# A hand-written first stage: statistics straight through on VectorE, its filler matmuls and GpSimd scalings left out

## The chip, the cores and the metric

The kernel runs on one core of one Trainium2 chip. Times are device microseconds of one execution; a number for a kernel is the median of its runs. In the profile, PE is TensorE's matmuls and PEld its weight loads, DVE is VectorE, ACT is ScalarE, POOL is GpSimd and SP is the engine that issues most transfers.

## What is computed

A linear attention without softmax, normalised by its root mean square, and then an MLP mixer, all in fp32 (8 batches, 8 heads, 576 positions, head size 64; 256 token and 1536 channel features):

```python
kv  = np.einsum('bhsd,bhse->bhde', k, v)
out = np.einsum('bhsd,bhde->bhse', q, kv)
rms = np.sqrt(np.mean(out * out, axis=-1, keepdims=True) + 1e-06)
x   = out / rms * g_norm                      # then (B,H,S,D) -> (B, S, H*D)

h   = np.maximum(x.transpose(0, 2, 1) @ w_tok1, 0.0) @ w_tok2
u   = x + h.transpose(0, 2, 1)
out = u + np.maximum(u @ w_ch1, 0.0) @ w_ch2
```

The MLP weights come as 64-bit floats, which the kernel decodes to fp32 itself.

## The kernel before

**Stages.** Two batches make a pair, and there are four pairs. A first stage (the list `start`) does the attention of pair 0 and begins its token mixing. `middle` and two `steady` stages each interleave the attention of the next pair with the token mixing of the one before; `last` does the token mixing of pair 3. After that comes the channel MLP, by far the longest part, as an unbroken row of matmuls (ps_a, ps_b, ps_d and others), with fast matrix multiplication in sums and differences on VectorE.

**Order of the work.** The order is written out by hand. Each string of `start` is a list of step names, and `play` (L1192) calls them one after another; each call records instructions, and every engine executes its own in the order in which they were recorded. Instructions of different engines wait for one another by semaphores where they share data or a buffer. A name in a list is a letter and numbers:

- `kvSH`: k by v of side S (the batch within the pair), half H (four heads), 20 matmuls of 64 columns into ps_kv; `eSH`: its eviction to kvp (`evict`, L379 to 385). In pair 0 the eviction takes the whole 128x256 (the banks were zeroed ahead, so that two heads make a block-diagonal square) on VectorE, L383; in later pairs two 128x128 halves go on ScalarE, L130.
- `aCT`: attend, four matmuls q by kv of column group C (0 and 1 are side 0, 2 and 3 side 1, 4 the remainder of both), tile T of 128 positions, into ps_o (ps_r for the remainder), of which there are two banks.
- `gCT`: gain, VectorE, L444: x = bank times g_norm. `qCT`: square of the same bank, ScalarE, L448. `tCT`: sum over each head, VectorE, L465. `mC`: mean and epsilon, VectorE, L470. `rC`: root, ScalarE, L475. `iC`: inversion with one refining step, four small VectorE instructions, L479 to 484. The two readers of a bank, gain and square, stand in the order in which they were recorded: the second waits for the first.
- Scaling x by the inverse, in three forms: `sCT` on ScalarE (eight activations of 128x64, L498), `dCT` on VectorE (one, L502), `pCT` on GpSimd (one, L506).
- `h0TJ`: one matmul of token mixing's first product, 128x512 into ps_h, of side 0, feature half T, position tile J (tile J is x of group J // 2, tile J % 2). In `middle`, `h1T` are the four of side 1 at once, `hr` those of the remainder, `uI` the second product and its addition.
- `wNK`: steps of decoding a token weight; `lSH`, `lqS`, `lrS`: loads for the next pair; `jN`: N matmuls of the identity whose result nobody reads (`keep_warm`, ps_j; TensorE's pace in the first microseconds is lower).

All matmuls are recorded through one helper, L133; a matmul in fp32 shows as two records in the profile. Copies by ScalarE show as L130, transfers as L121. The steps that the change touches are the strings of `start`, `evict`, and the sizes for which `jN` exist; the second stage, whose first steps wait for x of groups 2 to 4, is the same text before and after.

**Transfers.** Loads go on SP's queue in recorded order; an issue waits for the eighth one ahead of it to have landed, and for the buffer (k and v of a pair's four parts have one buffer each, q two).

Of the kernel before, what the change touches and what calls it, by code (L numbers as in the profile page):

```python
# [20 lines left out]
def kernel(  # L21
# [90 lines left out]
    def do(f, *a, **kw):  # L112
        return lambda: f(*a, **kw)
# [15 lines left out]
    def copy(o, a):  # L129
        keep(nc.scalar.copy(o, a))  # L130
# [121 lines left out]
    def t_sums(b):  # L252

        def step(o, x, y):
            return lambda: tensor_add(b(o), b(x), b(y), ALU.subtract)

        return [step(5, 7, 1), step(6, 3, 5), step(7, 3, 7), step(4, 2, 6)]
# [96 lines left out]
    def attention(pair, groups):  # L354
# [7 lines left out]
        whole = pair == 0  # L362
# [16 lines left out]
        def evict(side, half):  # L379
            n = P if whole else D  # L380
            o, i = kvp[side][:, 2 * half:2 * half + 2, :n], kv_ps[side, half][:, :, :n]
            if whole:
                keep(nc.vector.tensor_copy(o, i))  # L383
            else:
                copy(o, i)
# [123 lines left out]
        for s in range(2):  # L509
            for h in range(2):  # L510
                steps |= {f"kv{s}{h}": do(kv, s, h), f"e{s}{h}": do(evict, s, h),
                          f"l{s}{h}": do(load, 4 * pair + 4 + 2 * s + h)}
            steps |= {f"lq{s}": do(load_q, 2 * pair + 2 + s), f"lr{s}": do(load_q_rest, 2 * pair + 2 + s)}
# [678 lines left out]
    def play(lines, after={}, **stages):  # L1192

        for name in " ".join(lines).split():
            if name.isdigit():
                for _ in range(int(name)):
                    next(stages["rounding"], lambda: None)()
            elif name[0] == "-":  # L1200
                stages["before"][name[1:]]()
            else:
                next(stages[s][name] for s in ("attention", "mixing", "more")
                     if name in stages.get(s, ()))()
# [28 lines left out]
    for block in tok1[2:] + tok2:  # L1233
# [6 lines left out]

    start = [
        "kv00 e00 l00 j14 w01 w11 w02 w03 w04 w12 w13 w14", "kv01 j10 e01 l01",
        "a00 g00 q00", "a01 g01 q01 t00", "a10 g10 q10 t01 m0 r0", "a11 g11 q11 t10 i0 p00 p01",
        "kv10 j6 t11 m1 r1 e10 i1 s10 p11", "kv11 j2 e11", "h000 h001 h002 h003", "a20 g20 q20", "a21 g21 q21 t20",
        "h010 t21 m2 r2", "a30 g30 q30 i2 p20", "a31 g31 q31 t30", "h011 t31 m3 r3 p21", "a40 i3 p30 g40 q40 p31",
        "h012 h013 t40 m4 r4 w21 i4 s40 lq0 l10 l11 lr0 lr1"]
    middle = [
        "kv00 e00 w31 w22 w23 w24", "h10 -lq1 w32 w33 w34", "kv01 e01 w41 w42",
        "h11 w43 w44", "hr l00", "a0 q00 g01 q01 g00 t00 t01", "u0 z2 f0", "u1 l01",
# [20 lines left out]
    more = {f"w{n}{k}": f for n, b in enumerate(tok1 + tok2) for k, f in enumerate(b)}  # L1270
# [6 lines left out]
    def keep_warm(n):  # L1277

        o = ps["h"].tile([P, DM], F32, name="ps_j", tag="h")
        for _ in range(n):  # L1280
            matmul(o[:, :P], lhsT=ident, rhs=ident, start=True, stop=True)

    more |= {f"j{n}": do(keep_warm, n) for n in (2, 6, 10, 14)}
    play(start, attention=attentions[0], mixing=mixings[0], more=more)
    play(middle, attention=attentions[1], mixing=mixings[0], before=attentions[0],
         more=more, rounding=rounding)
    for n in range(1, B // 2 - 1):
        play(steady[n - 1], attention=attentions[n + 1], mixing=mixings[n], before=attentions[n],
             more=more, rounding=rounding)
# [16 lines left out]
    more = {f"c{i}": f for i, f in enumerate(t_sums(lambda n: uT[0][:, SB[n]]))}  # L1306
# [97 lines left out]
```

## Time and profile before

| | us |
|---|---|
| median of 3 runs | 789.23 (788.98 to 789.61) |
| the profiled execution, its own time | 788.88 |
| span of its profile | 787.10 |
| TensorE busy in the span | 774.4 |
| VectorE busy | 612.9 |
| ScalarE busy | 265.4 |
| GpSimd busy | 78.3 |
| first stage ends on TensorE, next stage's first k by v starts | 39.79 |
| TensorE's last matmul ends | about 783.9 |

A line of a timeline reads: start in us from the span's start, length in us, engine, line, operation, what is written from what, sizes, how many; in brackets, how long the engine had been idle and what it waited for. A matmul's end is modelled, and matmuls overlap, so that start to start is the better measure of what one costs. A line of waits reads: who waited, for whom, us in total, how often, the longest. A line of stretches: the stretch and its length, then busy us (and instructions) of PE, PEld, DVE, ACT and POOL, the granted clock of TensorE, the mean share of 16 DMA engines, GB/s.

### The profile page before, as it was taken

Reading aid. Unit: us, or ns where it says so; the run is one execution under the profiler, and the core shown is the slowest. Engines: PE = TensorE matmul, PEld = TensorE weight load, DVE = VectorE, ACT = ScalarE, POOL = GpSimd, SP = SyncE. Lnnn points to the kernel's source line nnn. Section 1 sums busy time; section 2 is a strip of 40 time slices with the busy share of each in tenths; the row PEclk is TensorE's granted clock in tenths of the full one; section 3 lists DMA queues with packets and bytes.
Section 4 is the critical chain, followed back from the end, with each engine's and each line's share of the span. In section 5 each row is a group of like instructions: output and inputs, shape, how many; then the busy total and the mean of one; then the engine's idle time right before and its main releaser. Section 6 shows DMA issues by size and latency. Waiting matters only on the chain.

```text
span 787.1 us, 14853 instructions
## 1 busy us (share of the span) xinstructions
PE 774.4 (98%) x5832; PEld 652.6 (83%) x5832; DVE 612.9 (78%) x906; ACT 265.4 (34%) x513; POOL 78.3 (10%) x91
## 2 busy tenths in 40 slices
PE   6999999999999999999999999999999999999998
PEld 5655555544888888999988899998889999889998
DVE  2666887796776868988778889776898885787977
ACT  2356564846110133511133242123352113325211
POOL 1211212122410000010100001010000101000111
PEclk9999999999999999999999999999999999999999
DMA  9999999587699795599897579889559889655864
GB/s 295 327 334 371 361 371 344 212 268 282 235 292 337 269 339 148 154 309 205 246 236 231 151 218 272 247 203 290 148 158 283 206 222 230 200 153 151 200 173 91
DMA packets 132614, 192.12 MB, mean 244 GB/s; under 512 B 13633, under 2 KB 92225, under 8 KB 132545
## 3 DMA queue, kind: packets, MB, share of 16 engines
q1 hardware_dynamic: 115984, 167.54, 68.1%
q0 software_dynamic: 14656, 22.02, 13.7%
q10 hardware_dynamic: 1904, 1.61, 0.7%
q8 instruction: 46, 0.75, 0.4%
q14 instruction: 24, 0.19, 0.1%
HBM read 138.31 MB, written 52.82 MB: 243 GB/s over the span
## 4 chain that ended last, share of the span: by engine, by line
PE 95%; DVE 2%; ACT 1%; DMA 1%; issue 0%; SPq 0%; ACTq 0%
PE ps_d L133 28%; PE ps_b L133 19%; PE ps_a L133 19%; PE ps_h L133 8%; PE ps_u L133 8%; PE ps_v L133 5%; PE ps_c L133 3%; PE ps_kv L133 2%; PE ps_w L133 2%; PE ps_o L133 2%; DMA raw<-in_moe_w_tok_dram 1%; ACT x L498 1%; DVE x L444 0%; DVE ms L465 0%; PE ps_j L133 0%
## 5 line engine op out<-in xcount | busy, mean ns | idle before, releaser
L133 PE MATMUL ps_d<-ui,w 128*128 128x256 f32 x504 | 118.6, 379 | 0.0
L133 PEld LDWEIGHTS ps_d<-ui,w 128*128 128x128 f32 x504 | 95.1, 190 | 12.8 <-DVE v L124 0.2
L130 ACT COPY ps_d<-ps_a 128x768 f32<-128x768 f32 (+1 forms) x56 | 32.0, 571 | 215.6 <-PE ps_a L133 215.6
L124 DVE TENSOR_TENSOR v<-v,v 128x1536 f32<-128x1536 f32 (+2 forms) x70 | 103.5, 1483 | 0.3
L133 PE MATMUL ps_b<-w,sv 128*128 128x128 f32 x672 | 84.7, 276 | 0.0
L133 PE MATMUL ps_a<-w,v 128*128 128x128 f32 x672 | 84.2, 275 | 0.0
L133 PEld LDWEIGHTS ps_a<-w,v 128*128 128x128 f32 x672 | 79.9, 192 | 0.2
L133 PEld LDWEIGHTS ps_b<-w,sv 128*128 128x128 f32 x672 | 79.5, 192 | 0.2
L133 PE MATMUL ps_u<-h,w_tok 128*128 128x512 f32 (+1 forms) x160 | 67.2, 606 | 0.2
L133 PE MATMUL ps_d<-w,v 128*128 128x128 f32 x528 | 66.3, 275 | 0.0
L133 PE MATMUL ps_h<-x,w_tok 128*128 128x512 f32 (+1 forms) x160 | 65.5, 603 | 0.7 <-ACT x L498 0.7
L133 PEld LDWEIGHTS ps_d<-w,v 128*128 128x128 f32 x528 | 62.7, 192 | 0.3
L127 ACT ACTIVATE v<-v 128x768 f32<-128x768 f32 (+1 forms) x54 | 42.6, 821 | 55.1 <-DVE v L124 55.1
L133 PE MATMUL ps_d<-w,sv 128*128 128x128 f32 x480 | 60.1, 275 | 0.0
L133 PEld LDWEIGHTS ps_d<-w,sv 128*128 128x128 f32 x480 | 57.1, 192 | 0.2
L133 PEld LDWEIGHTS ps_h<-x,w_tok 128*128 128x128 f32 (+1 forms) x160 | 26.1, 189 | 32.7 <-issue 29.0
L1121 POOL DMA_DIRECT2D out_dram<-us x11 | 14.1, 1278 | 379.3 <-ACT us L130 347.4
L133 PEld LDWEIGHTS ps_u<-h,w_tok 128*128 128x128 f32 (+1 forms) x160 | 24.8, 179 | 31.0 <-issue 25.6
L133 PE MATMUL ps_a<-uT,w 128*128 128x256 f32 x192 | 46.7, 379 | 0.0
L444 DVE TENSOR_TENSOR x<-ps_o,g_sb 128x512 f32<-128x512 f32 x32 | 21.6, 687 | 28.6 <-PE ps_o L133 23.3
L133 PE MATMUL ps_b<-ui,w 128*128 128x256 f32 x168 | 40.8, 379 | 0.0
L133 PEld LDWEIGHTS ps_a<-uT,w 128*128 128x128 f32 x192 | 36.3, 190 | 4.8
(145 smaller groups left out, 1216.2 us busy)
## 6 DMA issues: line engine op xcount, KB each, us to landing
w<-parts SPq DMA_DIRECT2D x168, 384.0 KB, 4.1
w<-parts SPq DMA_DIRECT2D x56, 192.0 KB, 3.4
uT<-blocks SPq DMA_DIRECT2D x36, 256.0 KB, 5.7
k_in<-in_k_dram SPq DMA_DIRECT2D x16, 512.0 KB, 8.7
qT<-in_q_dram SPq DMA_DIRECT2D x8, 1024.0 KB, 9.2
out_dram<-x POOLq DMA_DIRECT2D x16, 512.0 KB, 6.1
v_in<-in_v_dram SPq DMA_DIRECT2D x14, 512.0 KB, 8.8
raw<-in_moe_w_ch_dram SPq DMA_DIRECT2D x8, 768.0 KB, 10.4
```

The lines of the kernel that those rows point to most:

```text
L124: keep(engine.tensor_tensor(out=o, in0=a, in1=b, op=op))
L127: keep(nc.scalar.activation(o, a, AF.Relu))
L130: keep(nc.scalar.copy(o, a))
L133: keep(nc.tensor.matmul(*a, **kw))
L444: keep(nc.vector.tensor_mul(x, bank[c, h], g_sb.to_broadcast([P, number(c), D])))
L498: keep(nc.scalar.activation(x[:, k, h], x[:, k, h], AF.Copy, scale=inv[:, k, h]))
L1121: keep(nc.gpsimd.dma_start(to.rearrange("t p e -> p t e"), a, accum_op=ALU.add))
```

## The change

- The second side's k by v (`e10`, `e11`) are evicted by ScalarE instead of VectorE, still as whole 128x256.
- In the first stage VectorE's instructions are recorded one pair of tiles after another, without those of the next between (gains, sums, mean, inversion, scaling), and from group 1 on with the square ahead of the gain of the same bank.
- Tiles 00 and 01 are both scaled by VectorE; in groups 1, 2 and 3 VectorE scales tile 0 and ScalarE tile 1. GpSimd scales none in this stage (seven before); ScalarE scaled 10 and 40 before, now 11, 21, 31 and 40.
- The filler `j6` and `j2` is gone; `j14` and `j10` stay.
- The first product's matmuls of the two feature halves are taken in turn, as each tile of x comes.

```diff
         def evict(side, half):
             n = P if whole else D
             o, i = kvp[side][:, 2 * half:2 * half + 2, :n], kv_ps[side, half][:, :, :n]
-            if whole:
+            if whole and side == 0:
                 keep(nc.vector.tensor_copy(o, i))
             else:
                 copy(o, i)
...
     start = [
         "kv00 e00 l00 j14 w01 w11 w02 w03 w04 w12 w13 w14", "kv01 j10 e01 l01",
-        "a00 g00 q00", "a01 g01 q01 t00", "a10 g10 q10 t01 m0 r0", "a11 g11 q11 t10 i0 p00 p01",
-        "kv10 j6 t11 m1 r1 e10 i1 s10 p11", "kv11 j2 e11", "h000 h001 h002 h003", "a20 g20 q20", "a21 g21 q21 t20",
-        "h010 t21 m2 r2", "a30 g30 q30 i2 p20", "a31 g31 q31 t30", "h011 t31 m3 r3 p21", "a40 i3 p30 g40 q40 p31",
-        "h012 h013 t40 m4 r4 w21 i4 s40 lq0 l10 l11 lr0 lr1"]
+        "a00 g00 q00", "a01 g01 q01 t00 t01 m0", "a10 q10 r0 i0 d00 d01", "a11 q11 g10 g11 t10",
+        "kv10 e10 t11 m1 r1", "h000 h010 h001", "kv11 e11 i1 d10 s11", "h011", "a20 q20",
+        "a21 q21 g20 g21 t20 t21 m2", "h002 h012 r2 i2 d20", "a30 q30 g30", "a31 q31 s21 g31 t30", "h003 h013 t31 m3",
+        "a40 q40 r3 i3 d30 s31 g40 t40 m4 r4 w21 i4 s40 lq0 l10 l11 lr0 lr1"]
...
-    more |= {f"j{n}": do(keep_warm, n) for n in (2, 6, 10, 14)}
+    more |= {f"j{n}": do(keep_warm, n) for n in (10, 14)}
```

## The prediction, made before the changed kernel ran

> **What bounds the kernel now.** I read the busy totals first, then all of TensorE's waits, a table of stretches, then TensorE's timeline around the change, and last the timelines of the other engines and the landing times of the transfers there.
>
> ```profile
> PE 774.4 (98%) x5832; PEld 652.6 (83%) x5832; DVE 612.9 (78%) x906; ACT 265.4 (34%) x513; POOL 78.3 (10%) x91
> ```
> TensorE is busy for 98% of the span. Its waits are few:
>
> ```profile
> PE ps_kv L133 <- DMA v_in<-in_v_dram: 6.2, 1, 6.2
> PE ps_kv L133 <- DVE w_tok L178: 1.1, 1, 1.1
> PE ps_o L133 <- ACT sq L448: 0.8, 2, 0.5
> PE ps_h L133 <- ACT x L498: 0.7, 1, 0.7
> PE ps_r L133 <- ACT sq L448: 0.2, 1, 0.2
> ```
> These are all, and but for 0.24 us at 71.6 all lie ahead of 37 us. The stretches confirm it (length, then busy time of PE, PEld, DVE, ACT and POOL):
>
> ```profile
> 21.87:39.79 17.92, 16.88 (x162) 11.54 (x161) 11.88 (x32) 6.41 (x18) 5.12 (x5) 1.00 1.09 329
> 37.40:784.00 746.60, 745.98 (x5526) 628.72 (x5522) 595.25 (x865) 254.65 (x489) 72.09 (x74) 1.00 0.82 241
> ```
> From 37.4 to 784 us TensorE never stops. So what the first stage gives back reaches the end whole, unless a later producer has no slack; and even spare matmuls in the first stage cost their full time. There the timeline shows (start, length):
>
> ```profile
> 21.87 1.39 PE L133 MATMUL ps_kv<-v_in,k_in 128*64 128x64 f32 x40
> 23.19 1.60 PE L133 MATMUL ps_j<-ident 128*128 128x128 f32 x12
> 24.92 1.39 PE L133 MATMUL ps_kv<-v_in,k_in 128*64 128x64 f32 x40
> 26.24 0.71 PE L133 MATMUL ps_j<-ident 128*128 128x128 f32 x4
> 26.79 1.88 PE L133 MATMUL ps_h<-x,w_tok 128*128 128x512 f32 x4
> 29.40 1.98 PE L133 MATMUL ps_h<-x,w_tok 128*128 128x512 f32 x4 [0.73 <-ACT x L498]
> 36.85 1.09 PE L133 MATMUL ps_r<-kvp,qR 128*64 128x128 f32 x16 [0.18 <-ACT sq L448]
> 39.79 1.39 PE L133 MATMUL ps_kv<-v_in,k_in 128*64 128x64 f32 x40
> ```
> The ps_j are filler: j6 takes 23.19 to 24.79, then 0.13 passes to 24.92; j2 takes 0.55.
>
> [...] after a 1.14 us gap before 13.77 the same 40 matmuls still take 1.39 us, against 2.40 for the first ones. [...] while GpSimd scales (24.72 to 26.76), the tiny L470 takes 0.58 us instead of 0.17 and L480 0.43 instead of 0.18:
>
> ```profile
> 24.72 2.04 POOL L506 TENSOR_TENSOR x<-x,inv 128x512 f32<-128x512 f32 x2 [21.30 <-DVE inv L484]
> 25.22 0.58 DVE L470 TENSOR_SCALAR ms<-ms 128x16 f32<-128x16 f32 x1
> ```
> [...]
>
> **The change, part by part.** What goes, on TensorE between 21.87 and 39.79: j6 and j2, 1.60 + 0.13 + 0.55 = 2.28 us. Seven GpSimd scalings (1.02 us each) leave an idle engine: nothing by themselves. What comes: five VectorE scalings (0.69 alone, 0.61 apart when back to back, row L502), two more ScalarE scalings (2.02 each), and, in place of two VectorE evictions (about 0.4 each), two ScalarE evictions of 128x256, which the trace lacks. ScalarE copies of 128x128 take 0.24 to 0.27 and of 128x512 0.57 to 0.61, which puts 0.38 between them[...]. I take 0.40[...]. A gain from it is excluded below its own length.
>
> What decides is whether x is there when TensorE asks sooner. I walk the new order with lengths from this stage: half a k by v 1.32 start to start, one 128x512 matmul (an h) 0.91, two attend tiles 1.78, remainder 1.03; square 0.60; gain, scaling or sum 0.61 to 0.69; root 0.22; the four small steps of an inversion 0.96, starting 0.10 after the root; 0.03 from engine to engine, 0.05 to TensorE, 0.2 from TensorE's last matmul to a reader.
>
> Group 0: squares end at 19.84 and 20.74 as before; the sums go straight through, t01 to 21.45, mean 21.66, root 21.91 (q10, put ahead of it on ScalarE, ends 21.69), inversion 22.97, d00 23.69, d01 24.30. TensorE is free at 23.19 and waits for d00: **0.55 us**. Then h000, h010, h001 to 26.47; kv11 to 27.79 (its last transfer was what the 0.13 waited for; it is long there); h011 to 28.70.
> Group 1: g10 to t11 24.22 to 26.73, m1 26.94, root, i1 to 28.25, d10 28.97. The eviction e10 is put between squares and root with 3 us of room; e11 waits for kv11 and ends at 28.4, when a20 is asked for at 28.70: no wait[...]. Queued behind e11 are s11 (28.4 to 30.4) and behind that q20: so g20 starts only at 30.98.
> Group 2: a20, a21 to 30.48, h002, h012 to 32.30. Squares 30.95 and 31.45, g21 32.28, sums 33.47, i2 34.99, d20 35.71, with s21 on ScalarE 35.0 to 37.05. a30 needs only g20 (31.67): no wait; a31, h003, h013 to 35.90.
> Group 3: g30 stands behind d20: 35.63 to 36.32, and the remainder takes that bank: **0.47 us** of waiting. Remainder 36.37 to 37.40; the next stage's first k by v then starts at 37.4 instead of 39.79. i3 39.64, d30 40.36, s31 39.68 to 41.70. Of side 1's first four h only the last, asked for at 41.45, waits: **0.3 us**.
> After that s40 ends at 44.97, needed at 47.6; the second token weight is decoded by about 49.4, needed at 50.6 (ScalarE starts it at 45.0 instead of 45.76).
>
> Before, the filler, its gap and the old waits (0.73 and 0.18, 0.2 more where an h is slower than 0.91) are 3.4 us that were not work; after, 0.55 + 0.47 + 0.3 = 1.3. **Gain 2.1 us.** The clock times agree: 39.79 - 37.4 - 0.3 = 2.1.
>
> Transfers: SP's order is unchanged and GpSimd only loses work, so nothing queues behind something new. But DMA is saturated here (over 1.0 of 16 engines), so landings stay put while TensorE comes earlier. From issue plus landing time: second qT 18.26 + 9.7 = 28.0 against a need at 28.7; k and v for 37.4 at 34.9 and 36.7, the short v rows near 37.4 against a need near 37.9; the next v at 40.5, its short rows near 41.6, against 42.7. All fit, two by only 0.5 to 0.7. Later raw-weight loads hang on VectorE and TensorE releases and move along; where ScalarE waits 4.4 us for one (135.76), its next readers have 2 us of room.
>
> The profiled execution took 788.88 us, 787.10 of it span and 1.78 around it; 788.88 - 2.1 = 786.8. It lies 0.35 under the median, so on the median's footing 789.23 - 2.1 = **787.1**.
>
> **Rivals.** (1) *Absorbed.* A landing that TensorE now meets too early[...]: if one of the two tight transfers comes 1 us late, TensorE waits 0.5[...]. Either or both leave 0.3 or so: 788.9. For it: DMA saturation and margins of 0.5 us. Against: no gap in the walk exceeds 0.55, and the trace's 1.14 did no harm. (2) *The statistics chain becomes the bound and the kernel slower.* From d00 at 23.69 to s31 at 41.70 VectorE and ScalarE hand over in one unbroken chain, 18.0 us, and the last h already waits for it. Each us that it grows is a us at the end: at +2.1 the gain is gone, at +3.7 (a fifth) it is slower by 0.2%. With the 48 or so instructions on it 0.1 us longer each, +4.8: 789.23 - 2.1 + 4.8 = 791.9. For it: squares now come ahead of gains, so a bank is freed only after both, and s11 holds up q20. Against: every length is measured in this stage[...]. (3) *It does not do what it says:* the built program shows 24 fillers instead of 32, no GpSimd scaling in the first stage, and the squares ahead of the gains from group 1 on; I give this nothing.
>
> **How the numbers follow.** Gain of 1.6 to 3.2: 0.68, likeliest 787.1; 3.2 is all the waits gone (786.0), hardly to be reached. Absorbed: 0.24, 788.9. Chain-bound: 0.08, 791.9. A change under 0.2%, 1.6 us, can't be told from none here, so faster 0.68, same 0.24, slower 0.08. Range 786.2 to 789.2: it covers the likeliest with its bounds and nearly all of the absorbed case.
>
> **What would show it.** The next stage's first k by v at 37.4; waits of TensorE of 0.5 for a VectorE scaling at 23.2, 0.5 for a gain at the remainder, 0.3 for a ScalarE scaling near 41.5; L470 at 0.18 throughout; s31 ending at 41.7. I am wrong if s31 ends past 43, if a transfer releases TensorE between 28 and 44, or if the stretch from 44 us on is no longer free of idle time.

## The result and the profile after

| | before | after |
|---|---|---|
| median, us (10 runs each, in turn) | 789.28 (788.77 to 789.98) | 787.37 (786.71 to 788.51) |
| the profiled execution, its own time | 788.88 | 787.48 |
| span of its profile | 787.1 | 785.7 |
| next stage's first k by v starts | 39.79 | 37.22 |
| next stage's token mixing (h1) starts on TensorE | 46.05 | 43.95 |

The ratio is 0.9977, 95% interval 0.9967 to 0.9987: the changed kernel is faster by 1.9 us, and by 1.40 us where the two profiled executions are compared. The busy totals of the changed kernel:

```profile
PE 773.3 (98%) x5816; PEld 651.6 (83%) x5816; DVE 614.8 (78%) x909; ACT 269.5 (34%) x531; POOL 71.3 (9%) x84
```
GpSimd lost the seven scalings, 7 us, and that says nothing about the end: TensorE is still 98% busy. What it waits for in the changed kernel:

```profile
PE ps_kv L133 <- DMA v_in<-in_v_dram: 6.2, 1, 6.2
PE ps_o L133 <- ACT sq L448: 0.8, 2, 0.5
PE ps_u L133 <- ACT ps_u L130: 0.7, 1, 0.7
PE ps_kv L133 <- DVE w_tok L178: 0.5, 1, 0.5
PE ps_h L133 <- DVE x L502: 0.4, 1, 0.4
PE ps_r L133 <- DVE x L444: 0.2, 1, 0.2
PE ps_h L133 <- ACT x L498: 0.2, 1, 0.2
```
The last three are the forecast waits of the first stage. The third, on ps_u, was not forecast. TensorE's timeline in the changed kernel shows where each lies:

```profile
22.05 1.39 PE L133 MATMUL ps_kv<-v_in,k_in 128*64 128x64 f32 x40
23.86 2.84 PE L133 MATMUL ps_h<-x,w_tok 128*128 128x512 f32 x6 [0.43 <-DVE x L502]
28.91 1.95 PE L133 MATMUL ps_o<-kvp,qT 128*128 128x128 f32 x16
36.29 1.09 PE L133 MATMUL ps_r<-kvp,qR 128*64 128x128 f32 x16 [0.22 <-DVE x L444]
37.22 1.35 PE L133 MATMUL ps_kv<-v_in,k_in 128*64 128x64 f32 x40
41.58 1.12 PE L133 MATMUL ps_h<-x,w_tok 128*128 128x512 f32 x2 [0.20 <-ACT x L498]
43.95 5.62 PE L133 MATMUL ps_h<-x,w_tok 128*128 128x512 f32 x16
149.33 1.98 PE L133 MATMUL ps_u<-h,w_tok 128*128 128x512 f32 x4 [0.66 <-ACT ps_u L130]
```
The h1 of the kernel before, and the stretch from there to TensorE's last matmul:

```profile
46.05 5.62 PE L133 MATMUL ps_h<-x,w_tok 128*128 128x512 f32 x16
46.05:784.00 737.95, 737.33 (x5428) 623.81 (x5424) 589.79 (x847) 250.16 (x474) 68.35 (x70) 1.00 0.82 240
```
and the same stretch of the changed kernel:

```profile
43.95:782.50 738.55, 737.44 (x5428) 623.80 (x5424) 589.38 (x847) 250.88 (x479) 68.55 (x70) 1.00 0.82 241
```
From the h1 on TensorE is idle for 738.55 - 737.44 = 1.11 us; before it was 737.95 - 737.33 = 0.62. So the front of the kernel ends 46.05 - 43.95 = 2.10 us sooner, and a part is lost again later, at the new wait of 0.66 at 149.33: 2.10 - 0.66 = 1.44, and the profiled executions differ by 1.40.

VectorE's timeline in the changed kernel:

```profile
21.66 0.17 DVE L470 TENSOR_SCALAR ms<-ms 128x16 f32<-128x16 f32 x1
23.11 1.29 DVE L502 TENSOR_TENSOR x<-x,inv 128x512 f32<-128x512 f32 x2
30.86 1.42 DVE L444 TENSOR_TENSOR x<-ps_o,g_sb 128x512 f32<-128x512 f32 x2 [1.89 <-ACT sq L448]
```
L470 takes 0.17 to 0.18 us everywhere in this stage, with no GpSimd beside it; the two scalings of group 0 start at 23.11 (forecast 22.97), and the gains of group 2 wait 1.89 us for the squares, as foreseen.

The wait at 149.33 leads to ScalarE. Its timeline in the changed kernel, first in the new stage and then ahead of the wait:

```profile
23.48 0.37 ACT L130 COPY kvp<-ps_kv 128x256 f32<-128x256 f32 x1 [0.66 <-PE ps_kv L133]
28.33 2.02 ACT L498 ACTIVATE x<-x,inv 128x64 f32<-128x64 f32 x8
39.51 2.02 ACT L498 ACTIVATE x<-x,inv 128x64 f32<-128x64 f32 x8 [1.02 <-DVE inv L484]
136.68 1.17 ACT L163 ACTIVATE w_ch<-raw 128x1024 f32<-128x1024 f32 x1 [7.44 <-DMA raw<-in_moe_w_ch_dram]
148.71 0.57 ACT L130 COPY ps_u<-x 128x512 f32<-128x512 f32 x1
```
At 136.68 ScalarE has stood for 7.44 us behind a transfer of raw weights; it then has to catch up with the work queued behind, and L130, which copies x into a bank of ps_u ahead of the second product's matmuls there, ends at 149.28, 0.66 us late for TensorE. Before, the same instruction began at 135.76, after 4.42 us, and no one waited. So TensorE was 2.1 us sooner and this transfer 0.9 later. SP's queue, in the kernel before:

```profile
118.53 8.47 SPq L121 DMA_DIRECT2D blocks<-w_ch  x8
127.10 5.38 SPq L121 DMA_DIRECT2D raw<-in_moe_w_ch_dram  x5
```
and in the changed kernel:

```profile
121.13 8.66 SPq L121 DMA_DIRECT2D blocks<-w_ch  x8
129.99 3.85 SPq L121 DMA_DIRECT2D raw<-in_moe_w_ch_dram  x5
```
The load is issued from 129.99 on instead of 127.10, 2.9 us later, behind eight stores of decoded blocks that are also later. The order of the queue is the same; its transfers didn't follow TensorE. Its being later doesn't need TensorE's lead, though: e1, below, has the load at 129.88 with TensorE no sooner than before.

### The profile page after: what moved, and what is told of

It is laid out like the page before. It is cut to its first block, busy times and chain, and to the rows that moved or that the text cites. A ratio compares the mean times of both kernels' runs of the same rounds, so it can differ in the third digit from the quotient of the medians.

```text
span 785.7 us, 14826 instructions
## 1 busy us (share of the span) xinstructions
PE 773.3 (98%) x5816; PEld 651.6 (83%) x5816; DVE 614.8 (78%) x909; ACT 269.5 (34%) x531; POOL 71.3 (9%) x84
## 4 chain that ended last, share of the span: by engine, by line
PE 92%; ACT 3%; DVE 2%; DMA 2%; issue 0%; SPq 0%; ACTq 0%; DVEq 0%
PE ps_d L133 28%; PE ps_b L133 19%; PE ps_a L133 19%; PE ps_u L133 7%; PE ps_h L133 6%; PE ps_v L133 5%; PE ps_c L133 3%; PE ps_w L133 2%; PE ps_o L133 2%; PE ps_kv L133 2%; DMA raw<-in_moe_w_tok_dram 1%; ACT x L498 1%; DMA raw<-in_moe_w_ch_dram 1%; DVE ms L465 1%; DVE x L444 1%; ACT sq L448 1%
## 5 line engine op out<-in xcount | busy, mean ns | idle before, releaser
L130 ACT COPY ps_d<-ps_a 128x768 f32<-128x768 f32 (+1 forms) x56 | 32.0, 571 | 215.3 <-PE ps_a L133 215.3
```

## The experiments

Each kernel ran on one chip beside the kernel before. e1 to e4 shared a chip (before: 789.09, 42 runs), then e5 to e8 (789.24, 49 runs), then e9 to e11 (789.24, 27 runs). Where a start of "the h1" is given, it is the instruction that the table above has at 46.05 and 43.95; where a part is judged by it, that is one profiled execution of each kernel.

**e1: the kernel before without its filler.** Is the removed filler worth what its length says?

```diff
-        "kv10 j6 t11 m1 r1 e10 i1 s10 p11", "kv11 j2 e11", "h000 h001 h002 h003", ...
+        "kv10 t11 m1 r1 e10 i1 s10 p11", "kv11 e11", "h000 h001 h002 h003", ...
```


> The kernel before without the filler of 6 and 2 matmuls, nothing else. My theory: the filler stood in time in which TensorE had to wait anyway. Without it the second half's k by v still waits for its v to land (about 24.8), and the third h still waits for the ScalarE scaling that ends at 29.35, so nothing behind moves: 789.2, between 788.8 and 789.6. Rival (filler costs its full time wherever it stands, as the prediction's account of 2.28 us of filler has it): 787.0.

Measured: 789.42 us (13 runs), ratio 0.9998 (0.9989 to 1.0006). Nothing. In six of these runs TensorE's mean clock was 0.997 or 0.998, in the 42 of the kernel before beside them 0.999 or more; the other seven have a median of 789.10, so without those six there is no gain either. TensorE's timeline in e1:

```profile
24.68 1.39 PE L133 MATMUL ps_kv<-v_in,k_in 128*64 128x64 f32 x40 [1.16 <-DMA v_in<-in_v_dram]
26.07 2.12 PE L133 MATMUL ps_h<-x,w_tok 128*128 128x512 f32 x4
29.65 1.98 PE L133 MATMUL ps_h<-x,w_tok 128*128 128x512 f32 x4 [1.45 <-ACT x L498]
40.04 1.39 PE L133 MATMUL ps_kv<-v_in,k_in 128*64 128x64 f32 x40
```
Where the filler was, TensorE now waits for the v rows of the second half's k by v (kv11), and then 1.45 us for ScalarE's scaling of tile 10 (s10). The h that needs it starts at 29.65, where before it started at 29.40 (the stage began 0.26 later in this execution). The filler only filled time that these two waits set. SP's queue in e1, at the load that the result above is about:

```profile
129.88 4.17 SPq L121 DMA_DIRECT2D raw<-in_moe_w_ch_dram  x6
```

**e2: the changed kernel with the filler put back.**

```diff
-        "kv10 e10 t11 m1 r1", "h000 h010 h001", "kv11 e11 i1 d10 s11", ...
+        "kv10 j6 e10 t11 m1 r1", "h000 h010 h001", "kv11 j2 e11 i1 d10 s11", ...
```


> The changed kernel with the filler of 6 behind the third k by v and of 2 behind the fourth, as before. My theory: 2.15 us of filler first fill the three new waits of the first stage (0.43, 0.22, 0.20), and then push all that follows by about 1.3; of that up to 0.66 comes back from a wait near 149 us that a later TensorE meets less. 788.4, between 787.8 and 788.9. Rival (the two fillers cost their full time): 789.5. Rival (the gain came from the order of the statistics alone, and filler is free): 787.4.

Measured: 788.44 us, ratio 0.9989 (0.9982 to 0.9995). The h1 starts at 45.27, 1.3 us later than without. Of the three waits that the filler was to fill, only the 0.43 is gone; 0.21 and 0.20 stand behind it as before. In the new order the same filler costs time, in the old it costs none; what comes right behind it decides.

**e3: the changed kernel with the second side's eviction on VectorE again.**

```diff
-            if whole and side == 0:
+            if whole:
```


> The changed kernel with the second k by v evicted by VectorE again. My theory: on VectorE the second eviction stands ahead of group 1's inversion and waits for the fourth k by v (its end near 28.1), so the inversion begins at about 28.5 instead of 27.28, and the chain of statistics behind it is 1.2 us later to its end: 788.4, between 787.9 and 788.9, the h behind group 3's ScalarE scaling waiting 1 us or more. Rival (a 0.4 us eviction is hidden on either engine): 787.4.

Measured: 787.64 us, ratio 0.998 (0.997 to 0.9989); I expected 788.4, and 787.64 lies below the range given. In the first stage the theory held in part: the inversion of group 1 starts at 28.32 instead of 27.28, the remainder waits 0.79 us instead of 0.22, the h1 starts at 44.80, 0.85 later; but the h behind group 3's ScalarE scaling waits 0.20, not 1 us or more. The medians differ by 0.3, within the intervals, the profiled executions by 0.6: in the profile of e3 the wait at 149 is gone. A delay of the front is partly paid back where the front's lead had been lost anyway.

**e4: the changed kernel with one raw load ahead of two stores.** The raw load at 129.99 (step f8) goes in front of the stores b10 and b11 on SP.

```diff
-        "u6 t30 t31 m2 r2 i2 d20 p21 s30", "u7 1 d31 1", "u8 1 b10 b11"], [
-        "kv00 kv01 e00 e01 1 -d40 f8", ...
+        "u6 t30 t31 m2 r2 i2 d20 p21 s30", "u7 1 d31 1", "u8 1 f8 b10 b11"], [
+        "kv00 kv01 e00 e01 1 -d40", ...
```


> The changed kernel with one load of raw channel weights issued ahead of eight small stores of transposed blocks on SP's queue instead of behind them. In the changed kernel's profile ScalarE waits 7.4 us for that load (to 136.68), and TensorE 0.66 us near 149 for what ScalarE does behind it. My theory: that wait is what the end got less than the first stage gave; with the load earlier it goes, 786.7, and the runs spread less. Rival (DMA is the limit there and the next load is late instead, or the stores are missed): 787.4 or later.

Measured: 787.47 us, ratio 0.9974 (0.9964 to 0.9983). The wait at 149 is gone, but the time missed the expected 786.7. It is as long as the rival said, but not for its reason: no new wait of TensorE appears behind 45 us. In its profiled execution the front was later, by 0.5 us at the start of the stage, and TensorE lost 0.89 more where the next stage's first k by v waited for v_in at 38.77; the h1 starts at 45.03, 1.1 later than in the changed kernel, which alone could have ended the wait at 149. The wait for v_in is for the tight transfer of the prediction, met in this execution and not in the one above.

**e5: the changed kernel with the scaling engines of before.** Everything else as changed; GpSimd takes its seven scalings back.

```diff
-   ... "a10 q10 r0 i0 d00 d01", ...
-   ... "kv11 e11 i1 d10 s11", ... "h002 h012 r2 i2 d20", ... "a31 q31 s21 g31 t30", ... "... r3 i3 d30 s31 ..."
+   ... "a10 q10 r0 i0 p00 p01", ...
+   ... "kv11 e11 i1 s10 p11", ... "h002 h012 r2 i2 p20", ... "a31 q31 p21 g31 t30", ... "... r3 i3 p30 p31 ..."
```


> The changed kernel with x scaled by the engines of before: GpSimd for 00, 01, 11, 20, 21, 30 and 31, ScalarE for 10 and 40; order of the statistics, evictions and filler stay changed. My theory: the order of the statistics makes the gain, not the engine that scales. VectorE gets 0.6 us back for each of five scalings, which makes up for GpSimd's longer 1.02 us: the first h starts 0.3 later, the chain's end is no later: 787.6, between 787.2 and 788.1. Rival (GpSimd's scalings[...] were the cost before): 788.6 or more.

Measured: 787.75 us (12 runs, 786.12 to 789.81), ratio 0.9979 (0.997 to 0.9988): no difference from the changed kernel can be told. TensorE waits 0.82 us for GpSimd's first scaling, against 0.43 for VectorE's, and is no later behind it: the waits of 0.22 and 0.20 don't come, the k by v of the next stage starts at 37.23, the h1 at 43.82. VectorE's timeline in e5:

```profile
40.44 0.98 DVE L470 TENSOR_SCALAR ms<-ms 128x8 f32<-128x8 f32 x1
```
the same step in the changed kernel:

```profile
41.42 0.17 DVE L470 TENSOR_SCALAR ms<-ms 128x8 f32<-128x8 f32 x1
```
and GpSimd's timeline in e5:

```profile
39.35 2.04 POOL L506 TENSOR_TENSOR x<-x,inv 128x512 f32<-128x512 f32 x2 [2.02 <-DVE inv L484]
```
L470 takes 0.98 us beside GpSimd's two scalings, which end at 41.39, and 0.17 in the four other places of e5's first stage, where none runs. What stretches it is not shown. It ends at 41.42, when the same step of the changed kernel only starts, and so its length costs nothing here.

**e6: the changed kernel with 8 matmuls of filler fewer ahead of the attention.** The filler shrinks from 2.50 to 0.71 us; if TensorE may ask up to 1.8 us sooner for everything, does the end follow?

```diff
-        "kv00 e00 l00 j14 w01 ...", "kv01 j10 e01 l01",
+        "kv00 e00 l00 j14 w01 ...", "kv01 j2 e01 l01",
```


> The changed kernel with 2 matmuls of filler instead of 10 behind the second k by v, so that TensorE asks for everything about 1.7 us sooner. My theory: transfers limit the front of the changed kernel, and little of this arrives: new waits for q, k or v appear between 20 and 40 us, or the one near 149 grows; 787.1, between 786.7 and 787.6. Rival (the chain of statistics is what still binds, and it starts 1.7 us sooner): 785.7.

Measured: 787.34 us (22 runs), ratio 0.9979 (0.9972 to 0.9986): no difference from the changed kernel. TensorE's timeline in e6:

```profile
16.87 2.02 PE L133 MATMUL ps_o<-kvp,qT 128*128 128x128 f32 x16 [0.75 <-DMA qT<-in_q_dram]
35.73 1.09 PE L133 MATMUL ps_r<-kvp,qR 128*64 128x128 f32 x16 [0.22 <-DVE x L444]
37.58 1.39 PE L133 MATMUL ps_kv<-v_in,k_in 128*64 128x64 f32 x40 [0.76 <-DMA v_in<-in_v_dram]
43.84 5.62 PE L133 MATMUL ps_h<-x,w_tok 128*128 128x512 f32 x16
```
Of the 1.8 us, 0.75 goes at once into a wait for qT. The remainder is 0.56 us sooner than in the changed kernel, and then TensorE waits 0.76 for v_in; the h1 starts 0.1 sooner. In this execution the front is at the pace of its transfers.

**e7: e6, with two loads moved.** The two loads of the second token weight, which stood ahead of the second pair's k and v, go behind the load l01; and f8 goes early, as in e4.

```diff
-    for block in tok1[2:] + tok2:
+    for block in tok1[2:]:
...
-        "kv00 e00 l00 j14 w01 ...", "kv01 j10 e01 l01",
+        "kv00 e00 l00 j14 w01 ...", "kv01 j2 e01 l01 w30 w40",
```


> As e6_after_short_filler, and with two changes in the order of loads: the second token weight (1.2 MB, not needed before 44 us) goes behind the next pair's first k and v instead of ahead of them, and the load that ScalarE waits for at 136 goes ahead of eight stores, as in e4_after_early_load. My theory: if it is the order of arrivals that limits, TensorE's lead now gets through: 786.2, between 785.5 and 787.0. Rival (all of the transfers together are too slow, and something else is late instead): 787.2 or more.

Measured: 786.62 us (5 runs, 786.12 to 786.98), ratio 0.9964 (0.9952 to 0.9976). The lowest median of the study, 2.6 us under the kernel before, on few runs. TensorE's timeline in e7:

```profile
36.82 1.33 PE L133 MATMUL ps_kv<-v_in,k_in 128*64 128x64 f32 x40
43.55 5.62 PE L133 MATMUL ps_h<-x,w_tok 128*128 128x512 f32 x16
```
There is no wait for v_in here and none at 149; the one for qT is still there, 0.93 us. The h1 starts 2.50 us sooner than before, and the profiled execution, 786.39, is 2.49 shorter: the lead arrives whole.

**e8: the changed kernel once more,** to see how far its waits are its own.

> The changed kernel as it is, a second profile of it. My theory: the first stage takes the same time to 0.2 us, and the wait near 149 comes out anywhere between 0 and 1.5 us with the moment at which the load lands that ScalarE waits for: 787.4. Rival (that wait is a fixed cost of the change): 0.6 to 0.7 again.

Measured: 787.24 us, ratio 0.998 (0.9971 to 0.9989), the result again. But the waits of its profiled execution differ from those above: 0.41 us for v_in ahead of the next stage's first k by v (at 37.55), none at 149, where ScalarE's transfer had landed for 136.05. The two waits for transfers come and go between executions of one kernel. Those for VectorE, 0.42 and 0.22, are there again; the 0.20 for ScalarE is not, since TensorE comes later behind the wait for v_in.

**e9: the kernel before with TensorE's new order alone.** VectorE, ScalarE and GpSimd keep their instructions in their order; no filler; both feature halves of the h for tiles 0 and 1 go ahead of the second side's attend tiles, and those for tiles 2 and 3 behind. Unlike in the changed kernel kv11 stays ahead of all of them. Against e1 the order of the h is the only difference.

```diff
-        "kv10 j6 t11 m1 r1 e10 i1 s10 p11", "kv11 j2 e11", "h000 h001 h002 h003", "a20 g20 q20", "a21 g21 q21 t20",
-        "h010 t21 m2 r2", "a30 g30 q30 i2 p20", "a31 g31 q31 t30", "h011 t31 m3 r3 p21", "a40 i3 p30 g40 q40 p31",
-        "h012 h013 t40 m4 r4 w21 i4 s40 lq0 l10 l11 lr0 lr1"]
+        "kv10 t11 m1 r1 e10 i1 s10 p11", "kv11 e11", "h000 h010 h001 h011", "a20 g20 q20", "a21 g21 q21 t20",
+        "h002 h012 t21 m2 r2", "a30 g30 q30 i2 p20", "a31 g31 q31 t30", "h003 h013 t31 m3 r3 p21", "a40 i3 p30 g40 q40 p31",
+        "t40 m4 r4 w21 i4 s40 lq0 l10 l11 lr0 lr1"]
```


> The kernel before, VectorE's, ScalarE's and GpSimd's instructions as they were, without the filler of 6 and 2, and with TensorE's h in the order of the changed kernel: both feature halves of tiles 0 and 1 ahead of the second side's attend tiles, those of tiles 2 and 3 behind them. My theory: what counts is that TensorE no longer stands at the third h until ScalarE has scaled tile 10 (29.35): it does 2 h and the attend tiles meanwhile. First attend tile of side 1 at 29.7 instead of 31.2, next stage's first k by v at 37.9 to 38.1 instead of 39.8; 787.6, between 787.2 and 788.2. Rival (the straight order of the statistics on VectorE is the gain, and TensorE's order only follows it): 789.0 or more.

Measured: 788.09 us (22 runs), ratio 0.9981 (0.9974 to 0.9988). TensorE's timeline in e9:

```profile
25.15 1.39 PE L133 MATMUL ps_kv<-v_in,k_in 128*64 128x64 f32 x40 [1.97 <-DMA v_in<-in_v_dram]
26.47 3.70 PE L133 MATMUL ps_h<-x,w_tok 128*128 128x512 f32 x8
30.01 1.95 PE L133 MATMUL ps_o<-kvp,qT 128*128 128x128 f32 x16
38.03 1.33 PE L133 MATMUL ps_kv<-v_in,k_in 128*64 128x64 f32 x40
44.24 1.12 PE L133 MATMUL ps_h<-x,w_tok 128*128 128x512 f32 x2
```
Although TensorE waits 1.97 us for a transfer, more than in e1, none of the eight h waits any more, and the h1 starts at 44.24: 1.8 of the change's 2.1 us, with none of its edits on other engines. In e1 it starts at 46.30. The medians show less, 1.15 of the change's 1.9 to 2.0 us; the profiled execution has a wait at 149 too (0.55), and in four of the 22 runs the mean clock was 0.998.

**e10: the reverse, the changed kernel with TensorE's old order.** All four h of the first half stand in a row behind kv11.

```diff
-        "kv10 e10 t11 m1 r1", "h000 h010 h001", "kv11 e11 i1 d10 s11", "h011", "a20 q20",
-        "a21 q21 g20 g21 t20 t21 m2", "h002 h012 r2 i2 d20", "a30 q30 g30", "a31 q31 s21 g31 t30", "h003 h013 t31 m3",
-        "a40 q40 r3 i3 d30 s31 ..."]
+        "kv10 e10 t11 m1 r1", "kv11 e11 i1 d10 s11", "h000 h001 h002 h003", "a20 q20",
+        "a21 q21 g20 g21 t20 t21 m2", "h010 r2 i2 d20", "a30 q30 g30", "a31 q31 s21 g31 t30", "h011 t31 m3",
+        "a40 q40 h012 h013 r3 i3 d30 s31 ..."]
```


> The changed kernel with VectorE's, ScalarE's and GpSimd's instructions as they are and TensorE's h in the order of before: four h of one half ahead of the second side's attend tiles, the other half's one by one behind them. My theory: the third h waits for d10 and the fourth for s11 (30.4), the first attend tile of side 1 starts at 31.3 as before, and since squares now go ahead of gains and groups straight through, group 2 comes later than before: next stage's first k by v at 41.3, 790.6, between 789.6 and 791.2. Rival (the order of the statistics is the gain): 787.4 to 788.0.

Measured: 792.47 us, ratio 1.0032 (1.0019 to 1.0044), slower than before, and by more than I expected (5 runs). TensorE's timeline in e10:

```profile
25.61 1.39 PE L133 MATMUL ps_kv<-v_in,k_in 128*64 128x64 f32 x40 [1.83 <-DMA v_in<-in_v_dram]
29.36 1.12 PE L133 MATMUL ps_h<-x,w_tok 128*128 128x512 f32 x2 [0.45 <-DVE x L502]
30.68 1.12 PE L133 MATMUL ps_h<-x,w_tok 128*128 128x512 f32 x2 [0.20 <-ACT x L498]
39.03 1.43 PE L133 MATMUL ps_r<-kvp,qR 128*64 128x128 f32 x16 [1.93 <-DVE x L444]
40.39 3.29 PE L133 MATMUL ps_h<-x,w_tok 128*128 128x512 f32 x4
```
TensorE has less to do between the second side's attend tiles than in the changed kernel, and the bank for the remainder, freed by a gain that stands behind scaling d20 on VectorE, is 1.93 us late. The last line is longer than it should be (four such records take 1.88 to 1.98 elsewhere). The stretches of e10 show why; the granted clock is the figure behind the five engines:

```profile
38.00:40.00 2.00, 0.97 (x14) 0.97 (x16) 2.00 (x4) 1.70 (x8) 0.00 (x0) 0.91 1.12 307
40.00:42.00 2.00, 2.00 (x8) 0.89 (x5) 1.54 (x7) 0.70 (x2) 0.00 (x0) 0.50 1.06 338
42.00:44.00 2.00, 2.00 (x15) 0.73 (x15) 1.97 (x4) 1.72 (x8) 0.00 (x0) 0.74 1.06 366
```
The clock was halved for a while: 2.00 x (0.09 + 0.50 + 0.26) = 1.7 us lost. The profiled execution took 792.67; without this, 791.0. The two executions of e10 whose mean clock was 1.0 took 790.75 and 791.0, inside what I had expected (789.6 to 791.2).

**e11: the changed kernel with both moves of loads of e7,** its filler kept.

> The changed kernel with the two changes in the order of loads of e7_after_load_order and its filler of 10 kept. My theory: both waits for transfers (v at 37.5 in some executions, ScalarE's load at 136) are gone, and the whole of the first stage's 2.2 us arrives: 786.8, between 786.4 and 787.3, with a narrow spread. Rival (the load order does nothing by itself, the shorter filler made e7_after_load_order what it is): 787.4.

Measured: 786.9 us (5 runs, 786.71 to 787.09), ratio 0.9968 (0.9956 to 0.998). No wait for v_in ahead of the next stage's k by v and none at 149; the h1 starts at 44.10, 1.95 sooner than before, and the profiled execution, 786.90, is 1.98 shorter. The medians fall from the changed kernel (787.24, 787.37) over e11 to e7 (786.62), but the intervals overlap; what the profiles show is that in these executions the two waits for transfers are gone and nothing of the lead is lost.

## Why the prediction was right, point by point

Forecast 787.1, measured 787.37.

- **The walk through the first stage held.** Group 1 scaled on ScalarE from 28.4 (measured 28.33), g20 at 30.98 (30.86), group 3 on ScalarE from 39.68 (39.51), next stage's k by v at 37.4 (37.22). The three waits, forecast as 0.55, 0.47 and 0.3, were 0.43, 0.22 and 0.20, in the places and for the releasers named. L470 stayed at 0.17 to 0.18. The eviction that the trace lacked, taken as 0.40 from the copies that it has (128x128 0.26 on average, 128x512 0.58 to 0.60), took 0.37.
- **The sum.** From the third k by v (22.05, before 21.87) to the h1 the stage takes 21.90 us instead of 24.18, 2.28 less where 2.1 was forecast. Counted from start to start with the prediction's lengths (1.32 for half a k by v, 0.91 for an h), the waits cost 0.49, 0.27 and 0.35, in all 1.11 and not 1.3, and that is the difference. The profiled execution began the stage 0.18 later, which leaves 2.10; that this is the forecast to the digit is luck.
- **A step that failed: "Later raw-weight loads hang on VectorE and TensorE releases and move along; where ScalarE waits 4.4 us for one (135.76), its next readers have 2 us of room."** They did not move along. TensorE came 2.10 us sooner and the load 0.9 later; the room was used up and TensorE waited 0.66 us. That it is this load is shown by e7 and e11, whose front is as early (43.55 and 44.10): both issue it earlier, ScalarE starts on it at 130.90 and 131.06, and the wait is gone. (In e4 it is gone too, but there the front itself was 1.1 us later.) In e5 and e8, where ScalarE started at 135.34 and 136.05, there was none either; at 136.30 (e6) it was 0.37. That the load was later than in the profile of the kernel before needs no lead of TensorE: e1, with TensorE no sooner, issues it at 129.88, and ScalarE starts on it at 136.53. What sets its moment isn't settled; no run took that apart. The prediction had named this as a sign that it would be wrong ("the stretch from 44 us on is no longer free of idle time"): the sign came, and its size was small against the gain.
- **"All fit, two by only 0.5 to 0.7."** The first half of that was too sure. The v rows for 37.4 fit in the profiled execution, but came 0.41 us late in e8, the same kernel, and 0.89 in e4. The rival "absorbed" thus holds in part, in some executions. And three of e8's 20 runs (790.61, 790.65 and 791.58, against a median of 787.24) had a mean clock of 0.997 or 0.998. None of them was profiled, so where they lost it stays open.
- **Two sums that don't come out.** Of the rival "absorbed" the prediction says that "either or both" leave 0.3 us; by its own figures a transfer that comes 1 us late takes 0.5 and leaves 1.6, and that it could be as little as 0.3 was an estimate that no trace had shown. And with all waits gone the gain would be the 3.4 that it counts, not 3.2. Neither carries the forecast.
- **The chain-bound rival** did not come in the changed kernel. Its mechanism is real, though: in e10 a bank freed late by VectorE's gain holds TensorE for 1.93 us.
- **What the prediction had right as a sum and wrong as a cause.** It booked the gain as 2.28 us of j6 and j2 removed, less new waits, and read from TensorE's busy time that "even spare matmuls in the first stage cost their full time". The balance is true of TensorE's time, but that reading is wrong: removing the filler alone gives nothing (e1). Scaling without GpSimd gives nothing that could be told (e5), as the prediction had it. What makes the filler's time free is the order of the first product's matmuls: in the old order the third h stands ahead of the second side's attention and waits for tile 10's scaling, whatever stands before it. In the new order it stands behind two attend tiles. e9 has this and the missing filler alone and starts the h1 at 44.24, against 46.30 in e1; e10 has everything but this and is slower than before. So most of the gain doesn't need the statistics straight through on VectorE: with e9's order alone TensorE is within 0.3 us of the changed kernel at the h1. Whether they make the rest, up to 0.8 us in the medians, is not shown; the intervals overlap. The eviction on ScalarE is worth 0.85 us within the stage (e3), of which 0.3 shows in the medians, too little to be told.

## What to carry to other kernels

Busy time that nobody reads is worth removing only if what stands behind it on the same engine is ready: look up the next instruction's releaser first, and move the one that waits behind work that doesn't. When a gain is small against a kernel, follow it to the end: transfers with less slack than the gain take a part back in some executions, and loads that stand in the queue by their need keep it (e11 and e7, in their profiled executions; that their medians, 0.3 to 0.8 us lower, are really lower is not shown). Undo the parts one at a time, in both kernels, before naming one of them as the cause.

## What the runs showed of the hardware

- TensorE's clock fell in e10 behind a wait of 1.93 us: it was 0.91, 0.50 and 0.74 of full speed in the three stretches of 2 us from 38.00 on, which cost 1.7 us. In e9 a wait of 1.97 us, and in e10 itself one of 1.83, were followed by full speed, the next 40 matmuls taking 1.39 us as ever (granted 1.00 in each of e9's stretches from 21 to 35). Why the one wait was followed by a lower clock and the other two were not, no run shows.
- A kernel's executions can differ in their clock. The mean was under 0.999 in six of e1's 13 runs, four of e9's 22, three of e8's 20, one of e6's 22 and three of e10's five, all kernels without j6 and j2; in the 118 of the kernel before beside them, and in the 21 of e2, all with this filler, it never was, nor in the other 51 runs without it. Whether the filler makes this difference is not shown, since of the executions with the lower mean only e10's was profiled.
- When a transfer lands varies between executions of one kernel: ScalarE began on the raw load at 136.68 in one execution of the changed kernel and at 136.05 in another (e8), and between 135.34 (e5) and 137.01 (e3) in kernels that leave this load where it was. That is nearly the 2 us of room that the prediction gave it.
- In the front a landing stayed nearly where it was while TensorE came earlier: the short v rows of the next stage's first k by v were issued at 29.71 before and at 29.65 in the changed kernel, and took 7.4 and 7.9 us to land, while TensorE started on that k by v 2.57 us sooner.
- On SP's queue no issue in the traces of the kernel before and the changed kernel ends before the eighth one ahead of it has landed: in the kernel before the second qT goes out at 18.26, and the k issued at 11.40, eight ahead, took 6.8 us to land, until about 18.2.
